# Decoding weight words in PSUM instead of SBUF, and running a Newton iteration on GpSimd instead of VectorE, in an attention and MLP kernel

## The chip, the cores and the metric

The kernel runs on one core of a Trainium2 chip. The metric is the device time of one execution in microseconds (us). Profiles are one execution each, recorded by the hardware profiler. The engines are TensorE (PE in the profile; its weight loads are PEld), VectorE (DVE), ScalarE (ACT), GpSimd (POOL) and SyncE (SP, which here issues the DMAs). Lines such as L176 are lines of the kernel before; in the changed kernel lines behind the edits are 1 to 3 higher (L176 becomes L177, L179 L180, L401 L404).

## The reference

The input is q, k, v (8 × 8 heads, 576 tokens, 64 dims), gates f, a norm gain g, and two weight matrices (512 × 2048 and 2048 × 512) that arrive as 64-bit floats.

```python
cum = np.cumsum(np.log(np.clip(f, 1e-4, 1.0)), axis=-1)
scores = q @ k.T / 8 + (cum[..., :, None] - cum[..., None, :])   # causal
attn = softmax(scores) @ v
x = attn rearranged to (batch, 576, 512)
xn = (x - mean(x)) / sqrt(var(x) + 1e-6) * g
out = x + relu(xn @ w1) @ w2
```

## The kernel before

**Attention.** There are 64 heads. Each is done in four slots (t = 1 to 4) of growing query tiles, so there are 256 slots. A slot takes its pieces in the order of a string of letters (`ORDERS`), in which the engines' instructions are written out by hand: Q is the score matmuls (L357 to L360), S their mask and row minimum on VectorE (L383, which writes p in SBUF), e the exponential on ACT (L394), B the row sums' reciprocal on VectorE (L399, L400) and the scaling of p by it on GpSimd (L401). Two slots later p is transposed on TensorE (t, L407), copied by ACT (h, L457), and multiplied with v (A, L472 or L497). The first 16 heads work in plain fp32, later ones in two halves of reduced precision.

**MLP.** From slot 35 on, steps of the MLP run between the attention's pieces: mm1 (M, L576 to L578), relu on ACT (r, L584), its low part on VectorE (m, L589), mm2 (N, L598 to L600), for 18 chunks of 256 tokens with 16 steps each. mm2 accumulates in two PSUM banks of its own, acc0 and acc1, which are used by nothing before the first MLP step. All other PSUM tiles rotate through six banks (`bank`).

**Weights.** The weights have to be turned from 64-bit words into a high and a low part before the MLP can use them. Each matrix has 16 blocks, so there are 32 items n = 0 to 31, the two matrices alternately. `WPrep.tick` is called for one item after the other: about every 2.4 slots up to slot 34, then four times in five slots. For item n:

- `load`: SP's DMA brings the words (wr, 512 KB) to SBUF.
- `scaled` (L165): ACT writes the upper word as a float times 2^-112 into y.
- `decode`: VectorE masks the sign bit in place (L175), shifts y by 3 and ors the sign in (L176), and ors in three bits of the lower word (L179). All operands are in SBUF, and y is at the end the float weight w (tag `wy`, five buffers).
- `colsum` (TensorE, L191) and `centre` (VectorE, L199): for the first matrix, the norm's mean and gain are put into w.
- `high` (ACT cast, L215) and `low` (GpSimd subtraction, L219) make the two parts.

A tick calls high and low directly and puts decode and centre in a queue, from which the letters f, g and w in the slot's string take three, two and one. `scaled` of the next item stands in that queue as the sixth entry, so ACT gets it one tick ahead.

**The Newton iteration.** For each chunk, `chunk_rstd` (L639) makes the reciprocal square root of the tokens' variances: 2 operations to start and three steps of 4 on tiles of 128 × 2 (L643 to L651). These 14 operations go into a list, `later`, from which letter L takes 6 a slot (in the tail, 6 a step). `chunk_out` (L657) uses the result when the chunk's last mm2 is done.

## Time and profile before

| | us |
|---|---|
| three runs | 1245.64, 1245.47, 1249.25 (median 1245.64) |
| span of the profiled execution | 1248.5 |
| busy: PE, DVE, ACT, POOL | 1227.3, 819.2, 643.3, 407.7 |
| DMA | 100.45 MB, mean 80 GB/s |

The runs shown have no profile; the profiled execution is one more, 2.9 us longer in span than their median. In the rows of the prediction, a group's row (with bars) gives the busy time, the mean of one in ns, and the idle time ahead of it with its releaser. An instruction's own row (no bars) by source line gives the least, median and greatest duration in ns. A row of the timeline or the chain begins with the start and the duration in us, and may end with the idle time ahead of it in brackets. A row by window gives the window's length, then busy us and instruction counts of PE, PEld, DVE, ACT and POOL, then the granted TensorE clock (1.00 is full), the DMA share and GB/s.

### The profile page before, as it was taken

The page shows a single profiled execution, that of the slowest core. Times are in us where ns is not written, and L with a number is a line of the kernel's source. Part 1 is how long each engine was busy: PE and PEld are TensorE (multiplying, and loading weights), DVE is VectorE, ACT ScalarE, POOL GpSimd, SP SyncE. Part 2 cuts the span into 40 slices and gives each one's busy share as a digit, 9 for nine tenths or more (in the row PEclk, how much of TensorE's full clock was granted, in tenths as well). Part 3 has the DMA queues.
Part 4 walks back from the last instruction along what each step waited for, and adds up shares of the span by engine and source line. Part 5 has one row for each costly group of instructions (what it writes and reads, how often), then busy time and mean ns, then how long its engine had stood idle before and what let it go on. Part 6 is the DMA issues. An engine that isn't in the chain of part 4 may idle for free.

```text
span 1248.5 us, 25327 instructions
## 1 busy us (share of the span) xinstructions
PE 1227.3 (98%) x8368; PEld 1090.7 (87%) x8368; DVE 819.2 (66%) x2916; ACT 643.3 (52%) x1936; POOL 407.7 (33%) x513
## 2 busy tenths in 40 slices
PE   8898999999999999999999999999999999999998
PEld 6566887899999899999999999999999999999997
DVE  6678777378686868686868677777777773233232
ACT  6676565455555555555555555555555542112111
POOL 3444344334344344333343444343433320000000
PEclk9788998999999999999999999999999999999999
DMA  6354451132323222222222222222232301110100
GB/s 187 112 144 146 140 145 59 48 93 76 93 74 91 76 79 72 75 89 80 89 81 82 83 76 88 82 67 79 71 93 76 94 33 38 48 39 17 51 26 27
DMA packets 91252, 100.45 MB, mean 80 GB/s; under 512 B 26864, under 2 KB 76016, under 8 KB 91120
## 3 DMA queue, kind: packets, MB, share of 16 engines
q1 hardware_dynamic: 91120, 98.82, 26.1%
q8 instruction: 67, 1.10, 0.4%
q14 instruction: 65, 0.53, 0.1%
HBM read 79.61 MB, written 19.17 MB: 79 GB/s over the span
## 4 chain that ended last, share of the span: by engine, by line
PE 90%; DVE 5%; ACT 1%; DMA 1%; issue 1%; POOL 0%; SPq 0%; DVEq 0%; POOLq 0%; ACTq 0%
PE h L576 11%; PE h L577 11%; PE h L578 11%; PE acc L598 11%; PE acc L599 11%; PE acc L600 10%; PE tr L407 7%; PE o L497 5%; PE s L359 3%; PE s L360 3%; PE s L357 3%; PE o L472 2%; PE xp L407 1%; DVE wy L179 1%; DVE wy L176 1%
## 5 line engine op out<-in xcount | busy, mean ns | idle before, releaser
L401 POOL TENSOR_SCALAR p<-p,st 64x64 f32<-64x64 f32 (+4 forms) x320 | 174.5, 550 | 499.0 <-DVE st L400 208.6
L576 PE MATMUL h<-x,w1h 128*128 128x256 f32 x1152 | 329.9, 286 | 0.4 <-ACT x L560 0.3
L577 PE MATMUL h<-x,w1h 128*128 128x256 f32 x1152 | 327.2, 284 | 0.1
L578 PE MATMUL h<-x,w1l 128*128 128x256 f32 x1152 | 325.9, 283 | 0.0
L584 ACT ACTIVATE hh<-h 128x256 fp32r<-128x256 f32 x288 | 110.7, 384 | 300.4 <-PE h L578 298.4
L589 DVE SCALAR_TENSOR_TENSOR hh<-h,hh 128x256 fp32r<-128x256 f32 x288 | 121.1, 420 | 165.3 <-ACT hh L584 160.4
L598 PE MATMUL acc<-w2h,hh 128*128 128x512 f32 x576 | 228.5, 397 | 0.0
L599 PE MATMUL acc<-w2l,hh 128*128 128x512 f32 x576 | 227.8, 395 | 0.0
L600 PE MATMUL acc<-w2h,hh 128*128 128x512 f32 x576 | 225.1, 391 | 0.2 <-DVE st L399 0.2
L576 PEld LDWEIGHTS h<-x,w1h 128*128 128x128 f32 x1152 | 219.6, 191 | 6.4 <-issue 1.0
L577 PEld LDWEIGHTS h<-x,w1h 128*128 128x128 f32 x1152 | 220.3, 191 | 5.0 <-DVE x L561 0.3
L394 ACT ACTIVATE p<-p,st 64x64 f32<-64x64 f32 (+4 forms) x320 | 178.3, 558 | 85.1 <-DVE st L383 83.9
L578 PEld LDWEIGHTS h<-x,w1l 128*128 128x128 f32 x1152 | 220.1, 191 | 0.0
L457 ACT CAST ph<-tr 64x128 fp32r<-64x128 f32 (+4 forms) x384 | 109.0, 333 | 115.1 <-PE tr L407 97.9
L407 PE MATMUL tr<-identr,p 128*128 128x128 f32 (+1 forms) x896 | 144.5, 278 | 11.8 <-POOL p L401 10.2
L407 PEld LDWEIGHTS tr<-identr,p 128*128 128x128 f32 (+1 forms) x896 | 101.9, 132 | 42.3 <-POOL p L401 22.6
L383 DVE CUSTOM_DVE_ANT_0 p<-s,mask 64x64 f32<-64x64 f32 (+4 forms) x320 | 130.3, 420 | 11.1 <-PE s L357 6.6
L600 PEld LDWEIGHTS acc<-w2h,hh 128*128 128x128 f32 x576 | 108.4, 188 | 25.5 <-DVE st L399 0.7
L598 PEld LDWEIGHTS acc<-w2h,hh 128*128 128x128 f32 x576 | 109.6, 190 | 14.1 <-issue 0.3
L462 DVE TENSOR_TENSOR ph<-tr,ph 64x192 fp32r<-64x192 f32 x192 | 57.8, 301 | 97.6 <-ACT ph L457 93.3
L599 PEld LDWEIGHTS acc<-w2l,hh 128*128 128x128 f32 x576 | 109.6, 190 | 11.8
L359 PE MATMUL s<-hi 128*128 128x288 f32 (+4 forms) x288 | 95.9, 355 | 0.0
(83 smaller groups left out, 1858.1 us busy)
## 6 DMA issues: line engine op xcount, KB each, us to landing
raw<-in_qk_dram SPq DMA_DIRECT2D x48, 576.0 KB
wr<-in_w_dram SPq DMA_DIRECT2D x32, 512.0 KB
vr<-in_v_dram SPq DMA_DIRECT2D x64, 160.0 KB
out_dram<-xt SPq DMA_DIRECT2D x36, 256.0 KB
xa<-xs SPq DMA_DIRECT2D x32, 160.0 KB
xb<-xs SPq DMA_DIRECT2D x32, 128.0 KB
xw<-xa SPq DMA_DIRECT2D x64, 64.0 KB
xw<-xb SPq DMA_DIRECT2D x48, 64.0 KB
```

The costliest lines, as they stand in the source:

```text
L359: mm(sp, h.hi[:, 0, q0 : q0 + m], h.hi[:, 1, a:z], start=True, stop=False)
L383: nc.vector.tensor_tensor_reduce(out=pt[:m, a:z], in0=sp, in1=mask[:m, off + a : off + z], scale=-SCALE, scalar=3.0e38 if i == 0 else st[: ...
L394: nc.scalar.activation(pt[:m, :w], pt[:m, :w], AF.Exp, bias=st[:m, i : i + 1], scale=-1.0, accum_out=st[:m, 2:3])
L401: nc.gpsimd.tensor_scalar(out=pt[:m, :w], in0=pt[:m, :w], scalar1=st[:m, 3:4], scalar2=1.0, op0=ALU.mult, op1=ALU.mult)
L407: nc.tensor.transpose(out_, in_, ident[:m, :m])
L576: mm(ph, w1h[:, k, fs], c.x[k][:, 0, :], start=(k == 0), stop=False)
L577: mm(ph, w1h[:, k, fs], c.x[k][:, 1, :], start=False, stop=False)
L578: mm(ph, w1l[:, k, fs], c.x[k][:, 0, :], start=False, stop=(k == KT - 1))
L589: nc.vector.scalar_tensor_tensor(out=h[:, 1, :], in0=ph, scalar=0.0, in1=h[:, 0, :].bitcast(F32), op0=ALU.max, op1=ALU.subtract)
L598: mm(c.acc[i], h[:, 0, ts_], w2h[:, j, :], start=(j == 0), stop=False)
L599: mm(c.acc[i], h[:, 0, ts_], w2l[:, j, :], start=False, stop=False)
L600: mm(c.acc[i], h[:, 1, ts_], w2h[:, j, :], start=False, stop=(j == FT - 1))
```

## The change

Three edits:

1. `scaled` writes y in PSUM: for items 0 to 14 in acc0 and acc1 alternately, from item 15 on in a rotating bank. The sign's or (L176) works on y in place in PSUM; the last bit operation (L179) reads the lower word from SBUF and y from PSUM, and writes w in SBUF. The borrowing of two MLP buffers in the first ticks (`W_BORROW`) is gone.
2. For items from 15 on, `scaled` is issued in the item's own tick, behind `high` and `low`, instead of from the queue one tick ahead.
3. The 14 Newton operations of each chunk (252 in all) are issued on GpSimd.

```diff
+W_ACC = 15
...
         def scaled(self, n):
...
-            if layer == 1 and self.tick_no < W_BORROW:
-                d["y"] = m2(f"wy{layer}_{j}", U32)
+            if n < W_ACC:
+                d["y"] = ps.tile([P, DM], F32, tag=f"acc{n % 2}", bufs=1, name=f"y{layer}_{j}")
             else:
-                d["y"] = wpool.tile([P, DM], U32, tag="wy", bufs=W_FLOAT, name=f"wy{layer}_{j}")
-            nc.scalar.activation(d["y"].bitcast(F32), d["hw"].bitcast(F32), AF.Copy, scale=2.0**-112)
+                d["y"] = bank(f"y{layer}_{j}")
+            nc.scalar.activation(d["y"], d["hw"].bitcast(F32), AF.Copy, scale=2.0**-112)
...
         def decode(self, n):
...
-            y, z, low = d["y"], d["hw"], d["lw"]
-            d["w"] = y.bitcast(F32)
+            y, z, low = d["y"].bitcast(U32), d["hw"], d["lw"]
+            w = wpool.tile([P, DM], U32, tag="wy", bufs=W_FLOAT, name=f"wy{layer}_{j}")
+            d["w"] = w.bitcast(F32)
...
                 lambda: ve.scalar_tensor_tensor(
-                    out=y, in0=low, scalar=29, in1=y, op0=ALU.logical_shift_right, op1=ALU.bitwise_or
+                    out=w, in0=low, scalar=29, in1=y, op0=ALU.logical_shift_right, op1=ALU.bitwise_or
                 ),
...
+            if on(t) and t >= W_ACC:
+                self.scaled(t)
             a = self.decode(t) if on(t) else []
...
-            if on(t + 1):
+            if on(t + 1) and t + 1 < W_ACC:
                 self.queue.insert(min(W_ASIDE, len(self.queue)), lambda: self.scaled(t + 1))
...
     def chunk_rstd(c):
...
-        ve = nc.vector
+        ve = nc.gpsimd
```

The order of TensorE's and SP's instructions does not change. On ACT, this is the place of the last items' scaling (y or wy of item 30, first matrix, block 15, and item 31, second matrix) among the casts (w1h, w2h), the copies of transposed p (ph) and an exponential (p). Before:

```order
L584 ACTIVATE hh_11_2279<-h_11_2253 128x256
L165 ACTIVATE wy_15_2283<-wr_15_2195 128x512
L215 CAST w1h<-wy_13_2018 128x4x128
L457 COPY ph_12_2241<-tr_4_2307 64x128
L457 COPY ph_12_2241<-tr_4_2307 128x3x128
L457 COPY ph_12_2241<-tr_4b 128x128
L394 ACTIVATE p_2_2299,st_2_2300<-p_2_2299,st_2_2300 128x320
L165 ACTIVATE wy_15_2326<-wr_15_2227 128x512
L215 CAST w2h<-wy_14_2222 128x512
```

Now:

```order
L587 ACTIVATE hh_11_2309<-h_11_2283 128x256
L216 CAST w1h<-wy_13_2062 128x4x128
L165 ACTIVATE y_15_2324<-wr_15_2221 128x512
L460 COPY ph_12_2271<-tr_4_2338 64x128
L460 COPY ph_12_2271<-tr_4_2338 128x3x128
L460 COPY ph_12_2271<-tr_4b 128x128
L397 ACTIVATE p_2_2330,st_2_2331<-p_2_2330,st_2_2331 128x320
L216 CAST w2h<-wy_14_2260 128x512
L165 ACTIVATE y_15_2362<-wr_15_2254 128x512
```

Each scaling stands behind the cast now, not ahead of it, and is issued in the tick of its own item instead of from the queue of the tick ahead.

On GpSimd, this is the end of the weights' work and the first chunk's Newton operations (sv and rs are the variances and the results, w1l and w2l the weights' low parts, p the softmax tiles). Before:

```order
L401 TENSOR_SCALAR p_3_2336<-p_3_2336,st_3_2337 128x448
L401 TENSOR_SCALAR p_4_2401<-p_4_2401,st_4_2402 128x576
L219 TENSOR_TENSOR w2l<-wy_14_2222,w2h 128x512
L219 TENSOR_TENSOR w1l<-wy_14_2133,w1h 128x4x128
L219 TENSOR_TENSOR w2l<-wy_15_2326,w2h 128x512
L219 TENSOR_TENSOR w1l<-wy_15_2283,w1h 128x4x128
L401 TENSOR_SCALAR p_0_175<-p_0_175,st_0_2433 64x64
```

Now, cut after the first Newton operation behind the low parts:

```order
L646 TENSOR_SCALAR sv_2173<-sv_2173 128x2
L647 TENSOR_SCALAR rs_2174<-sv_2173 128x2
L651 TENSOR_TENSOR rs_2174<-rs_2174 128x2
L652 TENSOR_TENSOR rs_2174<-rs_2174,sv_2173 128x2
L653 TENSOR_SCALAR rs_2174<-rs_2174 128x2
L654 TENSOR_TENSOR rs_2174<-rs_2174 128x2
L404 TENSOR_SCALAR p_4_2433<-p_4_2433,st_4_2434 128x576
L220 TENSOR_TENSOR w2l<-wy_14_2260,w2h 128x512
L220 TENSOR_TENSOR w1l<-wy_14_2227,w1h 128x4x128
L220 TENSOR_TENSOR w2l<-wy_15_2364,w2h 128x512
L220 TENSOR_TENSOR w1l<-wy_15_2326,w1h 128x4x128
L651 TENSOR_TENSOR rs_2174<-rs_2174 128x2
```

Six Newton operations stand ahead of p of tile 4, and six more between the four low parts and p of the next head's tile 0, of which the first is shown; the last two follow that head's tile 1.

On VectorE, this is the tick of item 30. Before, and then now:

```order
L175 TENSOR_SCALAR wr_15_2195<-wr_15_2195 128x512
L383 ISA p_2_2299,st_2_2300<-s_2_0_2297,mask 128x320
L383 ISA st_2_2300 128x1
L176 SCALAR_TENSOR_TENSOR wy_15_2283<-wy_15_2283,wr_15_2195 128x512
L179 SCALAR_TENSOR_TENSOR wy_15_2283<-wr_15_2195,wy_15_2283 128x512
L399 TENSOR_SCALAR st_2_2300<-st_2_2300 128x1
```

```order
L176 TENSOR_SCALAR wr_15_2221<-wr_15_2221 128x512
L386 ISA p_2_2330,st_2_2331<-s_2_0_2328,mask 128x320
L386 ISA st_2_2331 128x1
L177 SCALAR_TENSOR_TENSOR y_15_2324<-y_15_2324,wr_15_2221 128x512
L180 SCALAR_TENSOR_TENSOR wy_15_2326<-wr_15_2221,y_15_2324 128x512
L402 TENSOR_SCALAR st_2_2331<-st_2_2331 128x1
```

The rows keep their order; y is a PSUM tile of its own, and only the last of the three writes the SBUF tile wy.

## The prediction

> **What bounds the kernel now.** I read the page first. Three of its lines say where there is time to win: the engines' busy shares, the granted clock by slice (31.2 us each), and the chain that ended last.

> ```profile
> PE 1227.3 (98%) x8368; PEld 1090.7 (87%) x8368; DVE 819.2 (66%) x2916; ACT 643.3 (52%) x1936; POOL 407.7 (33%) x513
> PEclk9788998999999999999999999999999999999999
> PE 90%; DVE 5%; ACT 1%; DMA 1%; issue 1%; POOL 0%; SPq 0%; DVEq 0%; POOLq 0%; ACTq 0%
> ```

> TensorE idles 1248.5 − 1227.3 = 21.2 us in all. But "busy" doesn't mean at full clock: the second to sixth slice have a granted clock of 0.7 to 0.9. The busy time by windows splits the rest.

> ```profile
> 195.00:234.00 39.00, 35.88 (x227) 28.06 (x226) 22.29 (x83) 19.14 (x62) 13.88 (x18) 0.91 0.16 51
> 234.00:1209.00 975.00, 974.64 (x6773) 895.71 (x6772) 642.95 (x2326) 489.18 (x1468) 309.45 (x385) 1.00 0.23 71
> ```

> From 234 to 1209 us TensorE idles 0.36 us in 975, at full clock: no edit of another engine gains there. All that this change can win lies before 234 us, where the weights are decoded, or in the last few us. So I looked at the decode's instructions, by line and grouped.

> ```profile
> L176 DVE SCALAR_TENSOR_TENSOR wy<-wy,wr x32: 678/816/1737, 8.6 to 194.1; 128x512 uint32<-128x512 uint32 x32
> L179 DVE SCALAR_TENSOR_TENSOR wy<-wr,wy x32: 677/692/1645, 9.3 to 195.8; 128x512 uint32<-128x512 uint32 x32
> L176 DVE SCALAR_TENSOR_TENSOR wy<-wy,wr 128x512 uint32<-128x512 uint32 x32 | 31.0, 968 | 0.0
> L179 DVE SCALAR_TENSOR_TENSOR wy<-wr,wy 128x512 uint32<-128x512 uint32 x32 | 27.3, 853 | 0.6
> L561 DVE TENSOR_TENSOR x<-xr,x x72: 407/425/1203, 115.8 to 1197.4; 128x256 fp32r<-128x256 f32 x72
> L589 DVE SCALAR_TENSOR_TENSOR hh<-h,hh x288: 402/425/428, 124.8 to 1242.4; 128x256 fp32r<-128x256 f32 x144
> ```

> The same bit operation takes 0.68 us or up to 1.74. L561 and L589 tell why: equal shapes, equal medians, but L561 reads two SBUF operands and reaches 1203 ns, L589 reads one from PSUM and never passes 428 in 288 times. The long ones lie beside GpSimd work. So a VectorE operation with two SBUF inputs is held up by GpSimd, one with a PSUM input isn't. Above 0.69 the decode loses 31.0 + 27.3 − 64 × 0.69 = 14.1 us, 0.44 a weight.

> Some of that is on the chain (the first two and the last of five such pieces before 105 us):

> ```profile
> 31.19 1.64 DVE wy L179
> ...
> 42.65 1.65 DVE wy L179
> ...
> 100.80 1.64 DVE wy L179
> ```

> The five are 1.41 to 1.66 long; their excess is 8.00 − 5 × 0.69 = 4.6 us. Behind the one at 42.65, TensorE waits for the row sums and for p, and what comes after costs more than the wait:

> ```profile
> 42.87:46.28 3.41, 1.85 (x11) 0.60 (x12) 2.58 (x10) 2.62 (x9) 1.58 (x3) 1.00 0.02 3
> 46.28:60.05 13.77, 13.77 (x56) 9.77 (x57) 7.93 (x31) 7.75 (x26) 5.64 (x7) 0.51 0.41 122
> 73.74:77.15 3.41, 2.19 (x16) 1.30 (x16) 2.26 (x15) 2.01 (x7) 1.15 (x2) 1.00 0.63 223
> 77.15:87.39 10.24, 10.24 (x42) 6.97 (x42) 7.02 (x27) 5.60 (x19) 5.57 (x7) 0.50 0.26 74
> 104.50:114.74 10.24, 10.24 (x47) 7.55 (x45) 8.89 (x28) 5.63 (x19) 5.48 (x6) 0.50 0.57 163
> 32.63:36.04 3.41, 2.32 (x22) 1.62 (x23) 2.59 (x14) 2.42 (x9) 1.70 (x4) 1.00 0.57 199
> ```

> A stretch in which TensorE is busy for 1.85 or 2.19 us of 3.41 is followed by 10 to 14 us at half clock; one with 2.32 isn't. Between these lies an edge of about 0.65 to 0.68: a stall of half a microsecond more decides on ten microseconds.

> **The change part by part.** The sum is made against the profiled execution: 1248.5 us of span, 2.9 above the median of the runs shown (1245.64) and 0.75 below the highest (1249.25).

> *Contention, before 113 us.* With y in PSUM, L176 and L179 read one SBUF operand each, like L589, and should stay at 0.68. The mask (L175) keeps its form. Directly, 4.6 us on the chain go. What the half-clock stretches cost I take from the heads' pace, read at the start of each head's first exponential (ACT's timeline):

> ```profile
> 30.24 0.35 ACT L394 ACTIVATE p<-p,st 64x64 f32<-64x64 f32 x1
> 90.14 0.36 ACT L394 ACTIVATE p<-p,st 64x64 f32<-64x64 f32 x1
> 99.85 0.35 ACT L394 ACTIVATE p<-p,st 64x64 f32<-64x64 f32 x1
> 113.61 0.35 ACT L394 ACTIVATE p<-p,st 64x64 f32<-64x64 f32 x1
> ```

> An undisturbed head takes 99.85 − 90.14 = 9.71 us. The seven heads from 30.24 to 113.61 took 83.37; at 9.71 each it would be 67.97. So 15.4 us is the ceiling, stalls and half clock together. I don't take all: the stretches sit near the edge, and other waits (the mask's own contention, DMA) remain. I keep one stretch of 10.24 us at half clock, which costs up to 10.24/2 = 5.1: **−10.3 us**, between −15.4 and, if all three stretches stay, −4.6.

> Does an operand in PSUM cost something itself? L589 (425 ns with PSUM) against L561 (425 without) says no; that VectorE or ScalarE also write into PSUM here no row shows, so I allow 0 to 4 us. [...]

> *The same-tick scaling, 113 to 208 us (items 15 to 31).* The scaling moves from the tick before to the place just behind the high part's cast on ACT. VectorE's mask (L175) overwrites the words that the scaling reads, so it now waits for an ACT operation of its own tick; queued behind it on VectorE are the next S, the centring and the sums' reciprocals, for which TensorE waits.

> ```profile
> 140.00:186.00 46.00, 46.00 (x327) 37.56 (x326) 34.14 (x110) 28.69 (x84) 17.41 (x20) 1.00 0.51 143
> 186.00:208.00 22.00, 18.88 (x131) 14.60 (x130) 21.20 (x67) 13.66 (x44) 12.90 (x15) 0.97 0.21 65
> 144.79 0.70 DVE L175 TENSOR_SCALAR wr<-wr 128x512 uint32<-128x512 uint32 x1
> ...
> 185.21 0.44 DVE L175 TENSOR_SCALAR wr<-wr 128x512 uint32<-128x512 uint32 x1 [0.21 <-ACT wy L165]
> 189.86 0.50 DVE L175 TENSOR_SCALAR wr<-wr 128x512 uint32<-128x512 uint32 x1
> 189.98 0.62 ACT L215 CAST w1h<-wy 128x512 fp32r<-128x512 f32 x1 [1.18 <-DVE wy L199]
> ```

> At item 30 the mask's turn on VectorE is at 189.86, while ACT's cast, which itself waited 1.18 for VectorE's centring, ends at 190.60. The scaling behind it, about as long as the cast (0.62), would end near 191.2: a stall of 191.2 − 189.86 = 1.34 us. I expect that in the ticks with a layer-1 cast, about half; the others wait 0 to 0.6. From 140 to 186 TensorE is busy without a gap and VectorE idles 46.00 − 34.14 = 11.9 us. Eight masks lie in it, the first and the last of which are shown: 1.5 us of idle time a tick, to which the removed contention adds 0.44. So the stall is covered, if that time lies where it is needed: +0.5 us, with 0 and +4 as ends. If that cover is gone, it is the second rival below. Each y also takes one of the six rotating banks for a tick, so TensorE's next tiles can wait for the last bit operation; I put this into the same ends. The GpSimd lows and SP's loads keep their place, and the five SBUF words are taken one step later than before, so no wait is added there.

> *Around 186 to 208.* VectorE is the bound there (21.20 of 22.00). These are the last stalled bit operation and the first, of three, then the first and last of the twelve Newton pieces on the chain, p's scaling behind them, and GpSimd's queue just ahead:

> ```profile
> 187.11 1.50 DVE wy L179
> 194.18 1.40 DVE wy L176
> 199.37 0.09 DVE sv L643
> 206.84 0.16 DVE rs L649
> 207.42 0.32 POOL p L401
> 200.90 0.75 POOL L401 TENSOR_SCALAR p<-p,st 128x576 f32<-128x576 f32 x1 [2.78 <-DVE st L383]
> 205.33 1.26 POOL L219 TENSOR_TENSOR w1l<-wy,w1h 128x512 fp32r<-128x512 f32 x1
> ```

> Gone are the three excesses, 0.81 + 0.60 + 0.71 = 2.1 us (the middle one is 1.29 long), against one stall of 1.34. The Newton pieces, 5.7 us with the contention in them, leave VectorE. But they go into GpSimd's queue: six ahead of the p at 200.90, where 2.78 us of idle time take them in, the next six behind the four lows that end at 206.59, ahead of the p at 207.42. With 0.25 us an operation these six take 1.5. The p at 200.90 and the lows start earlier by at most the first six on VectorE (0.95 by the chain), so GpSimd is through at 206.59 + 1.5 = 208.1 or up to 0.95 before that, 207.1: as late as the 207.42 of before, now by GpSimd's own queue. Hence 0 for both together, with −3 and +3 as ends. How long a 128x2 operation takes on GpSimd no row shows. It is bounded below by the smallest GpSimd row (0.104), above by the 64x64 p (0.32 on the chain); I take 0.25, nearer to the large one, because half of them read two tensors.

> ```profile
> L876 POOL MEMSET const-float32-0.0<- 128x1 f32 x1 | 0.1, 104 | 0.2 <-issue 0.2
> 1237.12 0.16 DVE L643 TENSOR_SCALAR sv<-sv 128x2 f32<-128x2 f32 x1
> 1244.07 1.43 DVE L657 SCALAR_TENSOR_TENSOR xt<-acc,rs,xt 128x512 f32<-128x512 f32 x2 [0.96 <-PE acc L600]
> ```

> *The other 17 chunks and the tail.* TensorE has work without a gap, and six GpSimd operations (1.5 us a slot) fit before the next p: 0, up to +2. In the tail the 14 start at 1237.1; at 0.35 they take 4.9 us and, since they run six to a step, are over before 1244.07. If they weren't, each missing microsecond would show in full.

> Sum: −10.3 + 0.5 + 0 + 0 = −9.8: 1248.5 − 9.8 = 1238.7 from the profiled execution, 1235.8 from the median. I take 1237.5.

> **Rivals.** *The clock stays.* The half-clock stretches may need more than the removed stalls to vanish. [...] But another cause of the stretches (DMA, the work's mixture) would leave them in place: then only 4.6 − 0.5 remain, 1245.64 − 4.1 = 1241.5 to 1244.4 from the profiled span. Against it: all three stretches follow a gap. Chance 0.2.

> *Slower: the same-tick scaling stalls VectorE.* Items 15 to 31 are 17 ticks; with 1.35 us in eight and 0.5 in nine they lose 15.3, and the removed contention gives back 17 × 0.44 = 7.5. If what VectorE loses comes onto the path, +7.8, and one lost half-clock stretch, some 1.7 net, more; with the direct 4.6 before 113 us gone and no clock won: 1245.64 + 7.8 + 1.7 − 4.6 = 1250.5. It decides if the stall passes 1.9 us a tick (the idle 1.5 plus the relief), or sooner where the idle time comes after the work that TensorE needs. For it: 1.34 at item 30 in a stretch that VectorE bounds. Against: the other parity waits less, and 140 to 186 us has slack. Chance 0.11.

> *It doesn't do what it says.* The bit operations are held up with y in PSUM too (L589's proof is for its own types), or become dearer by as much as they gain: 1245.6. Chance 0.07.

> **How the numbers follow.** Forecast 0.62, rivals 0.2, 0.11 and 0.07. Low end: the full ceiling from the median, 1245.64 − 15.4 = 1230.2, and a little for the end of 186 to 208 (−1.2): 1229. High end: the first and third rivals lie below 1247, the slower one is left out. A measurement can tell some 0.3%, 3.7 us, from no change. Faster: the forecast (0.60 of its 0.62) and a fifth of the first rival, 0.64. The same: the rest of it, the third and a remainder, 0.24. Slower: 0.12.

> **What would show it.** Right: L176 and L180 with maxima near 0.7 us; granted clock above 0.9 in the second to fourth slice; the head starts at 30 and 113 us about 73 apart; from 234 on the same pace. The Newton lines appear on POOL with a mean of 0.1 to 0.35. Wrong: the bit operations still reach 1.6; or they are short, but half-clock stretches of 10 us remain behind other gaps; or VectorE idles before the mask with ACT's scaling as releaser in more than half of the 17 ticks; or p at the first chunk's end waits for Newton operations on POOL longer than 0.5 us; or TensorE waits for L180 through a bank.

## The result, and the profile after

| | before | after |
|---|---|---|
| median of 20 runs | 1248.70 us | 1240.19 us |
| lowest to highest | 1242.42 to 1258.26 | 1238.54 to 1248.09 |
| ratio | | 0.9945, 95% interval 0.9925 to 0.9965 |
| span of the profiled execution | 1248.5 us | 1237.4 us |

The change makes the kernel faster by 0.35 to 0.75%, some 4 to 9 us (8.5 by the medians). Single runs of the kernel before are spread over 16 us, so its three runs on record (median 1245.64) were low by chance; its profiled execution stood a little above the middle of the twenty, since a run's time lies some 2 us above its span (in the changed kernel 1239.64 for the span of 1237.4).

The page of the changed kernel, busy shares and granted clock:

```profile
PE 1216.3 (98%) x8368; PEld 1084.8 (88%) x8368; DVE 758.5 (61%) x2664; ACT 641.8 (52%) x1936; POOL 448.0 (36%) x765
PEclk9997998999999999999999999999999999999999
```

VectorE has 60.7 us less to do, GpSimd 40.3 more. TensorE's instructions are the same, but they were busy for 11.0 us less, which is the gain of the profiled execution: its idle time is as long as before, but less of its busy time is at half clock. Where, the windows say (busy us of PE, PEld, DVE, ACT, POOL, then the clock). Before:

```profile
39.00:78.00 39.00, 35.10 (x205) 23.49 (x205) 26.67 (x104) 27.39 (x89) 17.39 (x22) 0.81 0.45 133
78.00:117.00 39.00, 36.80 (x198) 24.90 (x197) 28.45 (x100) 26.45 (x85) 19.57 (x24) 0.75 0.45 126
117.00:156.00 39.00, 37.44 (x254) 30.57 (x253) 29.47 (x94) 23.18 (x70) 13.48 (x16) 0.96 0.49 149
156.00:195.00 39.00, 39.00 (x282) 31.88 (x282) 31.29 (x94) 26.74 (x80) 17.75 (x19) 1.00 0.45 129
```

Now:

```profile
39.00:78.00 39.00, 36.99 (x260) 24.09 (x258) 29.72 (x128) 34.28 (x113) 19.82 (x28) 1.00 0.53 156
78.00:117.00 39.00, 34.15 (x201) 24.11 (x201) 28.70 (x99) 26.59 (x84) 16.93 (x22) 0.82 0.55 160
117.00:156.00 39.00, 39.00 (x274) 32.68 (x273) 25.34 (x85) 22.34 (x68) 13.61 (x16) 1.00 0.38 108
156.00:195.00 39.00, 36.45 (x246) 28.65 (x245) 28.40 (x101) 25.61 (x75) 17.88 (x25) 0.96 0.40 119
234.00:1209.00 975.00, 975.00 (x6786) 898.36 (x6785) 600.94 (x2095) 486.08 (x1459) 349.62 (x607) 1.00 0.23 71
```

From 39 to 78 us the clock is full now. From 78 to 117 it is still low, and from 156 to 195 a loss is new; both lie in the stretch where the scaling is done in the item's own tick. Finer windows give the stretches at half clock. Before 234 us there were five of 13.8, 10.2, 10.2, 3.4 and 6.8 us, about 44 in all. Now there are five of 3.4 (from 11.6 us), 6.8, 6.8, 3.4 and 6.8, about 27 in all. Half of the difference of 17 us, as an estimate from these lengths, is 8.5 of the 11 us gained.

This is one execution. Seven experiments below decode the first 15 items in the same way. In three of their profiles (late items as before with Newton on GpSimd and on VectorE, and the scaling ahead of the casts with Newton on VectorE) the clock is 1.00 from 0 to 78 us. In two (the weights alone, and the scaling ahead of the casts) it is 0.85 and 0.84 from 39 to 78 us. With the scaling ahead and the mask's result in the new tile, two heads take 15.8 and 15.7 us, from 21.92 to 53.45, where those from 21.15 take 9.5 and 9.9 with late items as before. With the mask's result in the new tile alone, the sixth head starts at 58.54, with late items as before at 58.53. So the early loss hasn't gone from every execution.

The decode's instructions by line (least, median, greatest ns; the mask, the shift, the last operation), then the mask's group now and before:

```profile
L176 DVE TENSOR_SCALAR wr<-wr x32: 407/429/1507, 8.2 to 184.3; 128x512 uint32<-128x512 uint32 x32
L177 DVE SCALAR_TENSOR_TENSOR y<-y,wr x32: 683/692/699, 8.7 to 185.5; 128x512 uint32<-128x512 uint32 x32
L180 DVE SCALAR_TENSOR_TENSOR wy<-wr,y x32: 673/686/695, 9.4 to 186.3; 128x512 uint32<-128x512 uint32 x32
L176 DVE TENSOR_SCALAR wr<-wr 128x512 uint32<-128x512 uint32 x32 | 19.1, 598 | 11.3 <-ACT y L165 11.0
L175 DVE TENSOR_SCALAR wr<-wr 128x512 uint32<-128x512 uint32 x32 | 15.9, 496 | 0.5 <-ACT wy L165 0.4
```

Both operations with an operand in PSUM keep within 22 ns of their least time in all 64 cases; before they reached 1737 and 1645. The mask, with all in SBUF, still reaches 1507, and VectorE now idles 11.0 us ahead of it for ACT's scaling. The heads' starts (first exponential, on ACT) show both sides:

```profile
30.72 0.35 ACT L397 ACTIVATE p<-p,st 64x64 f32<-64x64 f32 x1
86.96 0.35 ACT L397 ACTIVATE p<-p,st 64x64 f32<-64x64 f32 x1
99.97 0.35 ACT L397 ACTIVATE p<-p,st 64x64 f32<-64x64 f32 x1
```

Six heads take 86.96 − 30.72 = 56.24 us, 9.37 each; before, the undisturbed pace was 9.71 and the real one 11.91. The head that started at 113.61 starts at 99.97, 13.6 us earlier, and that although the last of these heads takes 13.01. From there to the end of the span it was 1248.5 − 113.61 = 1134.9 us before and is 1237.4 − 99.97 = 1137.4 now: 2.5 us are given back.

### The profile page after: what moved, and what is told of

Its sections match the earlier page's. It is cut to its first block, busy times and chain, and to the rows that moved or that the text cites. A ratio compares the mean times of both kernels' runs of the same rounds, so it can differ in the third digit from the quotient of the medians.

```text
span 1237.4 us, 25314 instructions
## 1 busy us (share of the span) xinstructions
PE 1216.3 (98%) x8368; PEld 1084.8 (88%) x8368; DVE 758.5 (61%) x2664; ACT 641.8 (52%) x1936; POOL 448.0 (36%) x765
## 4 chain that ended last, share of the span: by engine, by line
PE 90%; DVE 3%; ACT 3%; DMA 1%; issue 1%; POOL 1%; SPq 0%; DVEq 0%; ACTq 0%; POOLq 0%
PE h L579 11%; PE h L580 11%; PE h L581 11%; PE acc L601 11%; PE acc L602 11%; PE acc L603 10%; PE tr L410 7%; PE o L500 6%; PE s L362 3%; PE s L363 3%; PE s L360 2%; PE o L475 2%; PE xp L410 1%; DVE p L386 1%; ACT p L397 1%
## 5 line engine op out<-in xcount | busy, mean ns | idle before, releaser
L404 POOL TENSOR_SCALAR p<-p,st 64x64 f32<-64x64 f32 (+4 forms) x320 | 169.6, 534 | 451.7 <-DVE st L403 156.0
L601 PEld LDWEIGHTS acc<-w2h,hh 128*128 128x128 f32 x576 | 109.5, 190 | 14.1 <-issue 0.3
L340 POOL TENSOR_TENSOR hi<-raw,hi 64x576 fp32r<-64x576 f32 x48 | 73.8, 1537 | 66.7 <-ACT hi L338 65.3
```

The lines of the kernel that those rows point to most:

```text
L404: nc.gpsimd.tensor_scalar(out=pt[:m, :w], in0=pt[:m, :w], scalar1=st[:m, 3:4], scalar2=1.0, op0=ALU.mult, op1=ALU.mult)
L601: mm(c.acc[i], h[:, 0, ts_], w2h[:, j, :], start=(j == 0), stop=False)
```

## How the new wait throws the clock

Item 15 is the first that is scaled in its own tick. The timelines of ACT, VectorE and GpSimd there:

```profile
90.02 0.60 ACT L216 CAST w2h<-wy 128x512 fp32r<-128x512 f32 x1
90.53 0.66 ACT L165 ACTIVATE y<-wr 128x512 f32<-128x512 f32 x1
```

```profile
91.22 1.51 DVE L176 TENSOR_SCALAR wr<-wr 128x512 uint32<-128x512 uint32 x1 [0.73 <-ACT y L165]
92.65 0.61 DVE L386 CUSTOM_DVE_ANT_0 p<-s,mask 128x448 f32<-128x448 f32 x1
```

```profile
91.19 1.26 POOL L220 TENSOR_TENSOR w1l<-wy,w1h 128x512 fp32r<-128x512 f32 x1
```

VectorE waits 0.73 us until the scaling is over. By then GpSimd has just begun a low, and the mask, which needs 0.41 alone, takes 1.51. Behind it on VectorE stands the softmax's minimum, for which TensorE waits. Item 17 has the same on VectorE. These are its mask and TensorE's two waits for the minimum, behind item 15 and behind item 17:

```profile
103.16 1.14 DVE L176 TENSOR_SCALAR wr<-wr 128x512 uint32<-128x512 uint32 x1 [0.58 <-ACT y L165]
```

```profile
93.33 1.25 PE L360 MATMUL s<-kl,xf 66*128 66x288 f32 x2 [1.19 <-DVE st L386]
104.76 1.12 PE L360 MATMUL s<-kl,xf 66*128 66x448 f32 x1 [2.63 <-DVE st L386]
```

The windows that follow are laid on the places where the clock changes:

```profile
86.65:90.06 3.41, 3.02 (x15) 1.43 (x16) 2.67 (x13) 3.17 (x14) 2.64 (x4) 1.00 0.20 61
90.06:93.47 3.41, 2.22 (x22) 1.42 (x22) 2.56 (x7) 1.70 (x6) 1.76 (x2) 1.00 0.57 178
93.47:100.30 6.83, 6.69 (x27) 4.75 (x29) 4.94 (x20) 4.41 (x14) 2.54 (x3) 0.50 0.65 179
100.30:103.71 3.41, 1.83 (x13) 1.19 (x13) 2.58 (x9) 3.33 (x13) 2.31 (x4) 1.00 0.21 45
103.71:110.53 6.82, 5.77 (x27) 4.21 (x29) 5.57 (x17) 3.44 (x11) 2.35 (x3) 0.50 0.57 180
```

One stretch of 3.41 us with 2.22 us of work is followed by 6.83 us at half clock; another with 1.83, by 6.82 at half. Each of these costs up to 3.4 us more than the wait itself, as an estimate (half of the stretch). In the first window the 1.19 us without work are TensorE's wait behind item 15, so there, by this trace, the late scaling and the mask that it sets beside a low throw the clock. The second is less clear: TensorE was out of work from 102.13 us, and of its 2.63 us only 0.58 + 0.73 = 1.31 are the wait and the longer mask. A short half-clock stretch near this place is also left where the scaling is done a tick ahead (the third experiment), so that the wait causes the second stretch is not shown.

## The experiments

All were timed in rounds against the kernel before; ratios are to it, with 95% intervals. Its medians in these rounds were 1248.87 for the first four, 1249.21 for the next four and 1250.80 for the last two.

**The weights alone: Newton back on VectorE.**

```diff
     def chunk_rstd(c):
...
-        ve = nc.gpsimd
+        ve = nc.vector
```

> The changed kernel with the Newton operations back on VectorE: the weights' edits alone. Theory (the gain is the decode's, before 113 us, and the Newton move is worth nothing): within 2 us of the changed kernel, 1238 to 1242, and the head starts before 90 us as in the changed kernel. Rival (VectorE relieved of 54 us of Newton work is the gain): 1246 or more.

Measured: 1242.33 us, 0.9966 (0.9939 to 0.9994). By the medians the decode's edits carry most of the gain. The median stands 0.3 above what the theory gave and 3.7 below the rival's.

**Newton alone**, the kernel before with that line on GpSimd.

> The kernel before with only the Newton operations moved to GpSimd. Theory: 1247 to 1250, within 0.3% of the kernel before, since from 234 us on TensorE never waits; at the first chunk's end GpSimd's queue replaces VectorE's. Rival (the Newton move is the gain): 1243 or less.

Measured: 1243.42 us, 0.9981 (0.9954 to 1.0008). By the interval it can't be told from no change; by the medians (5.5 us apart) it gains. It lies 3.6 us below the theory's range and 0.4 above the rival's, so both ranges are missed.

**Late items as before**: items 0 to 14 in PSUM, items 15 to 31 in SBUF and scaled one tick ahead.

```diff
         def scaled(self, n):
...
-                d["y"] = bank(f"y{layer}_{j}")
+                d["y"] = wpool.tile([P, DM], F32, tag="wy", bufs=W_FLOAT, name=f"wy{layer}_{j}")
...
-            w = wpool.tile([P, DM], U32, tag="wy", bufs=W_FLOAT, name=f"wy{layer}_{j}")
+            w = wpool.tile([P, DM], U32, tag="wy", bufs=W_FLOAT, name=f"wy{layer}_{j}") if n < W_ACC else y
...
-            if on(t) and t >= W_ACC:
-                self.scaled(t)
...
-            if on(t + 1) and t + 1 < W_ACC:
+            if on(t + 1):
```

> The changed kernel, but items 15 to 31 are decoded as in the kernel before: y in SBUF and in place, scaled one tick ahead. Theory (scaling in the same tick costs time: the mask waits 11.0 us for it in 16 ticks): the stretches at half clock behind these waits go, and the time is 1235 to 1238, 2 to 5 faster than the changed kernel, though contention of 0.44 us a weight is back. Rival (the wait is covered and the contention is the dearer one): 1240 to 1244.

Measured: 1231.61 us, 0.9882 (0.9848 to 0.9917): 8.6 us below the changed kernel, more than the theory gave. So what the change does to the late items loses as much as the whole change gains. The contention is back there; the shift's rows, late items and early ones in one kernel:

```profile
L177 DVE SCALAR_TENSOR_TENSOR wy<-wy,wr x17: 673/1025/1661, 92.0 to 177.6; 128x512 uint32<-128x512 uint32 x17
L177 DVE SCALAR_TENSOR_TENSOR y<-y,wr x15: 680/693/699, 8.7 to 87.0; 128x512 uint32<-128x512 uint32 x15
```

That is the change's first edit in one profile, by the same operation with and without PSUM. And it shows that contention behind 90 us is cheaper than what the change put in its place. One stretch at half clock, a short one, is left ahead of 113 us:

```profile
99.60:103.01 3.41, 1.65 (x14) 1.34 (x15) 3.34 (x12) 2.67 (x8) 2.44 (x4) 1.00 0.21 56
103.01:106.42 3.41, 3.41 (x23) 2.75 (x23) 3.38 (x10) 1.37 (x5) 1.54 (x3) 0.50 0.59 192
```

**The kernel before with filler on TensorE.** Two transposes more in each of 28 slots.

```diff
+    pad = ps.tile([P, DM], F32, tag="acc0", bufs=1, name="pad")
...
             piece(c)
+            if c in "QA" and 6 <= u < 34:
+                nc.tensor.transpose(pad[:, 0:P], ident, ident)
```

> The kernel before with two extra 128x128 transposes on TensorE in each of slots 6 to 33, whose results are used by nothing: VectorE's stalls stay, but TensorE idles less. Theory (short idle times under a busy share of about 0.66 throw the clock to one half, and that is most of the loss): fewer half-clock stretches before 113 us, the clock there above 0.92, and 1238 to 1246 in spite of up to 10 us of added TensorE work. Rival (only the stalls themselves cost, or the clock falls for another cause): 1249 to 1258.

Measured: 1245.21 us, 0.9971 (0.9945 to 0.9997): more work, less time. In its profile the contention is as before, and the clock is not (L177 is L176 of the kernel before, one line down):

```profile
L177 DVE SCALAR_TENSOR_TENSOR wy<-wy,wr x32: 673/890/1749, 8.6 to 184.2; 128x512 uint32<-128x512 uint32 x32
...
39.00:78.00 39.00, 34.78 (x261) 23.91 (x259) 31.28 (x117) 30.17 (x98) 20.12 (x26) 1.00 0.47 138
78.00:117.00 39.00, 34.84 (x240) 24.70 (x239) 33.49 (x108) 29.72 (x93) 19.92 (x23) 0.96 0.56 159
```

This profiled execution took 1240.34 us; 5 of the 12 runs stand between 1238.88 and 1240.36 with a mean clock of 0.996 or 0.997, the others between 1244.90 and 1249.66 with 0.986 to 0.990. So the filler takes most of the half clock away in some executions, not in all. The profiled one shows that with more work on TensorE the clock stays at 1.00 from 39 to 78 us and at 0.96 from 78 to 117 (0.81 and 0.75 before) while the stalls stay (up to 1749 ns), as the theory has it.

**The scaling ahead of the casts.** In the changed kernel, the two lines that call `scaled(t)` stand ahead of the calls of `high` instead of behind `low`.

```diff
+            if on(t) and t >= W_ACC:
+                self.scaled(t)
             if on(t - 2, 2):
                 self.high(t - 2)
...
-            if on(t) and t >= W_ACC:
-                self.scaled(t)
             a = self.decode(t) if on(t) else []
```

> The changed kernel with one thing moved: from item 15 on ACT's scaling stands ahead of the casts of its tick instead of behind them. Theory (the mask waits because the scaling stands behind a cast that waits for VectorE's centring): the idle time of VectorE before the mask falls from 11.0 us to under 5, and the time to 1234 to 1237. Rival (the same-tick dependency itself costs, wherever ACT has it): 1239 to 1242, the wait still near 10 us.

Measured: 1232.00 us, 0.9868 (0.9827 to 0.9908), 8.2 below the changed kernel and 2 below what the theory gave. The mask's group:

```profile
L176 DVE TENSOR_SCALAR wr<-wr 128x512 uint32<-128x512 uint32 x32 | 15.2, 474 | 2.6 <-ACT y L165 2.4
```

The wait falls from 11.0 to 2.4 us, and the mask itself from 598 to 474 ns in the mean. In the changed kernel 12 of the 17 late masks took more than 0.5 us, each of them beside a low; all 32 masks took 19.1 us there and take 15.2 here. So it is not the dependency on the same tick that costs, but its place behind the cast.

**The mask's result into the new tile.** The mask no longer overwrites what the scaling reads.

```diff
         def decode(self, n):
...
-            y, z, low = d["y"].bitcast(U32), d["hw"], d["lw"]
+            y, hw, low = d["y"].bitcast(U32), d["hw"], d["lw"]
...
-                lambda: ve.tensor_scalar(out=z, in0=z, scalar1=0x80000000, scalar2=None, op0=ALU.bitwise_and),
+                lambda: ve.tensor_scalar(out=w, in0=hw, scalar1=0x80000000, scalar2=None, op0=ALU.bitwise_and),
...
-                    out=y, in0=y, scalar=3, in1=z, op0=ALU.logical_shift_left, op1=ALU.bitwise_or
+                    out=y, in0=y, scalar=3, in1=w, op0=ALU.logical_shift_left, op1=ALU.bitwise_or
```

> The changed kernel, but the mask writes the sign bits into the new SBUF tile w instead of over the words that the scaling reads, so that it no longer waits for ACT; the shift-and-or reads them from there. Theory: what waits for ACT is now the shift, half a microsecond later, behind the softmax's minimum, so that S is not held up: the wait halves and the time is 1233 to 1238. Rival (the wait only moves to the shift and holds up what follows by as much): 1239 to 1242.

Measured: 1232.84 us, 0.9893 (0.9852 to 0.9933), 7.4 below the changed kernel by the medians and just below the theory's range. The wait for ACT, now ahead of the shift, is 1.0 us in 3 times. It shortens the wait in another way than the experiment before, and gains nearly as much.

**Both of these together.**

> Both: the mask writes into w, and the scaling stands ahead of the casts. Theory: no wait for ACT is left, no contention in the shifts, so it is the fastest: 1229 to 1233, at or below the kernel with late items in SBUF (1231.6). Rival (PSUM banks taken by y, or contention in the mask, bound it): 1235 or more.

Measured: 1232.12 us, 0.9898 (0.9851 to 0.9944): in the theory's range, but not the fastest. No wait for the scaling is left in its trace, and it is no faster than the scaling ahead of the casts alone, so removing the rest of that wait brought nothing that these runs can tell. These three kernels decode the late items in PSUM and stand at 1232.0 to 1232.8, within 1.3 us of the 1231.61 with late items in SBUF. So with the wait shortened, PSUM for the late items neither gains nor loses anything here that could be told from noise.

**The second edit alone**: the kernel before, items from 15 on scaled in their own tick, in SBUF.

```diff
+W_ACC = 15
...
+            if on(t) and t >= W_ACC:
+                self.scaled(t)
             a = self.decode(t) if on(t) else []
...
-            if on(t + 1):
+            if on(t + 1) and t + 1 < W_ACC:
```

> The kernel before with the second edit alone: y in SBUF as before, but from item 15 on scaled in its own tick behind the casts; Newton on VectorE. Theory (the same-tick scaling costs about 5 us by itself behind 86 us): 3 to 7 us slower than the kernel before. Rival (it costs only together with the PSUM banks): within 2 us of it.

Measured: 1251.48 us, 1.0035 (1.0002 to 1.0068), 2.3 above the kernel before by the medians, 4.4 by the ratio. VectorE idles 11.4 us ahead of the mask for the scaling, 17 times. It is the same wait without any decoding in PSUM, so the banks are not its cause.

**PSUM for the early items and nothing else**: late items as before, Newton on VectorE.

> The changed kernel with items 15 to 31 decoded as before and the Newton operations back on VectorE: what is left of the change is y in PSUM for the first 15 items. Theory (the decode's early part is the gain, some 10 us and more; Newton gives some 2): 1233 to 1238, 2 to 4 above the same kernel with Newton on GpSimd (1231.6). Rival (the Newton move is half of the gain): 1240 or more.

Measured: 1235.12 us, 0.9897 (0.9861 to 0.9933): 3.5 above the same with Newton on GpSimd, as the theory had it. This one part of the change makes more than the whole.

**The scaling ahead of the casts, Newton on VectorE.**

> The changed kernel with the scaling ahead of the casts and the Newton operations back on VectorE. Theory: 1233 to 1236, that is 1 to 4 above the same kernel with Newton on GpSimd (1232.0). Rival (without contention VectorE's Newton operations cost nothing): 1231 to 1233.

Measured: 1231.89 us, 0.9869 (0.9829 to 0.9909), the same as with Newton on GpSimd (1232.00): the rival held.

## Why the prediction was right, and where not

The prediction gave 1237.5 us, 1229 to 1247, faster. Measured were 1240.19 and faster. That the sum of −9.8 came so near to the measured −8.5 (of the medians) is partly luck. It had −10.3 for the early contention and +0.5 for the same-tick scaling. The early items in PSUM alone are worth 12.9 us by their ratio (8.4 to 17.4) and 15.7 by the medians, and the late scaling costs 8 and not 0.5. By the medians both terms were too small, and the two errors largely cancel. By its own steps:

**The base.** The sum of −9.8 was made from the profiled execution's span and then set between that and a median of three. With the 2.2 us that lie around the changed kernel's span, 1248.5 + 2.2 − 9.8 = 1240.9, next to the 1240.19 measured. The 1237.5 was low because of the median of 1245.64, which twenty runs put at 1248.70.

**Contention.** The mechanism was right. The shifts stay under 0.70 us (at most 699 and 695 ns, before 1737 and 1645). The price of a PSUM operand, for which I allowed 0 to 4 us, is not there: 0.692 and 0.686 are the medians now, where the least of L176 was 0.678 and the median of L179 0.692 before. No run shows the 4 us: the 64 operations take 44.0 us now and took 58.3 before; at the least times of before (0.678 and 0.677) they would take 43.4, so PSUM costs some 0.6 us in all, as an estimate from these.

**The clock.** Right in kind, and the larger part of the gain. The six heads of 9.37 us and the filler experiment say it from both sides. A gain of 10.3 was expected before 113 us; the head's start moved by 13.6. I had kept one half-clock stretch of 10.24 us for what remains. Ahead of 113 us three remain: one of 3.4 behind the start, at 11.6 us, and two of 6.8. The one at 93.5 comes from the new wait, which the sum had elsewhere. The signs agree only in part: the bit operations keep to 0.7 us and the heads are 69 us apart, but the fourth slice of the clock's row has 0.7, where above 0.9 was asked. The rival "the clock stays" fell.

The edge of 0.65 to 0.68 of a window, below which the clock was to fall, is not as sharp as the prediction took it. In the changed kernel a window with 72% of work was followed by half clock, while in the kernel before one with 68% was not:

```profile
171.97:175.38 3.41, 2.45 (x18) 1.51 (x18) 2.85 (x8) 2.47 (x6) 0.97 (x2) 1.00 0.41 133
175.38:178.80 3.42, 3.18 (x13) 3.06 (x14) 2.44 (x10) 1.55 (x7) 1.19 (x1) 0.50 0.66 225
```

What else decides stays open. In the twenty runs of the changed kernel the mean clock tells the time as well: 0.993 with 1238.5 to 1239.5, 0.984 with 1244.5 to 1244.7, 0.980 and 0.981 with 1248.0 and 1248.1.

**The same-tick scaling.** Here the step failed: "the stall is covered, if that time lies where it is needed: +0.5 us, with 0 and +4 as ends". The stall itself was rightly sized. I expected 1.34 us in about half of the ticks and 0 to 0.6 in the others; measured are 1.22 to 1.39 in five and 0.16 to 0.73 in eleven, 11.0 us in all, where the slower rival reckoned 15.3 in 17. The cover holds in part: from 117 to 156 us five masks waited, 2.5 us together, and TensorE never idled. But I placed items 15 to 31 behind 113 us and priced them by VectorE's idle time from 140 to 186. The masks of items 15 and 16 begin ahead of 113 us, at 104.39 and 110.72 in the kernel before and at 91.22 and 98.89 now, as do those of items 17 and 18 now. Behind item 15 TensorE has too little other work (2.22 us in the window of 3.41), and the wait is followed by half clock.

The experiments price it at 7.4 to 8.6 us on the medians in the changed kernel, and at 0.2 to 8.5 by the interval in the kernel before. The clock carries most of it: the median of the mean granted clock over the runs is 0.989 in the changed kernel, 0.994 to 0.995 in the three with Newton on GpSimd that shorten the wait, and 0.9965 with late items as before. Of a span of 1238 us, 0.005 is 6.2 us and 0.0075 is 9.3, as an estimate. The slower rival's price of 7.8 was thus nearly right, but its way was not: it added up VectorE's waits over 17 ticks, while here a few of them cost by what the clock does behind them. It lost to the early gain, for which the rival took the direct 4.6 us and no clock. And the mask's cost was assumed constant, while its mean rose from 496 to 598 ns: a low often starts behind the same cast as the scaling, and mask and low come together (behind the cast of 132.42 the low starts at 132.94 and the scaling at 132.95, and the mask at 133.62 takes 0.89). The sign that VectorE idles ahead of the mask in more than half of the 17 ticks came true, with 16. TensorE waited for the last bit operation once, for 0.5 us.

**Around 186 to 208, and Newton.** An operation on GpSimd was put at 0.25 us. The rows of the first chunk on GpSimd, the first two and one of each other kind:

```profile
189.08 0.22 POOL L646 TENSOR_SCALAR sv<-sv 128x2 f32<-128x2 f32 x1 [0.18 <-DVE sv L632]
189.39 0.19 POOL L647 TENSOR_SCALAR rs<-sv 128x2 int32<-128x2 int32 x1
189.66 0.19 POOL L651 TENSOR_TENSOR rs<-rs 128x2 f32<-128x2 f32 x1
```

One takes 0.19 to 0.22 and the next begins 0.27 to 0.31 later, so about 0.27 is its price in a row. On the chain, six of them stand between the last low and p, first, last and p:

```profile
197.53 0.16 POOL rs L651
...
198.85 0.11 POOL rs L652
...
199.03 0.32 POOL p L404
```

That is 1.5 us, as predicted, and my own sign that something would be wrong (p waits for Newton on GpSimd longer than 0.5 us) came true; it costs little because the other arrangement costs nearly as much. With Newton on VectorE and the scaling first, the chain in the same place reads

```profile
183.90 0.78 DVE rs L651
184.70 1.21 DVE rs L652
...
187.19 1.19 DVE rs L654
...
189.18 0.16 POOL p L404
```

The four lows begin at 183.37 there and p comes 5.81 us after. In the changed kernel, with Newton on GpSimd, they begin at 192.53 and p comes at 199.03, 6.50 after; with late items as before the two figures are 5.80 and 6.49. So GpSimd's queue is 0.7 us dearer at this place. Overall Newton's move gains 5.5, 2.1, 3.5 and −0.1 us in the four pairs of medians (alone; in the change; with late items as before; with the scaling first), and 2.4, 2.6, 1.9 and 0.1 by the ratios. By these the forecast 0 (−3 to +3) holds in all four. Whether it gains beside contention and nothing without is not settled, as the intervals are as wide as these differences. In the tail the 14 operations end at 1229.24, 3.8 us before the last output begins at 1233.04: nothing, as predicted.

**From 234 us on**: 0.00 us of idle TensorE in 975, against 0.36. Right.

## What to carry to other kernels

Look at the clock's row and the window ahead of each drop (3.41 us in these traces) before pricing a stall. In this kernel waits of 0.3 to 1.2 us on VectorE cost nothing from 117 to 156 us, where TensorE had work. Where TensorE ran dry and the clock halved behind it, a wait cost itself and, as an estimate, half of the stretch: up to 3.4 us for the 6.83 us behind item 15. Price a moved dependency at its worst place, the first item that uses it, not at the mean of the stretch with slack. A change of several edits can hide one that loses: two moved lines (the scaling ahead of the casts) bring the kernel from 1240.2 to 1232.0 us.

## What the runs showed of the hardware beyond that

```profile
92.78:96.19 3.41, 2.68 (x21) 2.02 (x20) 3.14 (x11) 1.85 (x6) 1.25 (x2) 1.00 0.71 180
```

- ACT's scaling into PSUM takes 628 ns (median, changed kernel), into SBUF it took 668 (kernel before).
